# Preparing nine weight blocks in the last steps of five pairs of heads and in the last pair, and not every four steps of the last three

## The chip, the cores and the metric

One core of a Trainium2 chip runs the whole program. The metric is the device time of one execution in microseconds, as the median of several runs. The engines are TensorE (PE: matrix products and transposes; PEld is its weight load), VectorE (DVE), ScalarE (ACT), GpSimd (POOL), and SyncE (SP), which issues the DMAs of this kernel.

## The reference

Three layers, one after the other, in float32:

```python
# attention: q, k, v are (2, 8, 768, 64), centroids (8, 16, 64)
q_assign = argmax(q_n @ c_n.T); k_assign = argmax(k_n @ c_n.T)      # nearest of 16 centroids
scores = where(q_assign == k_assign, scale * q @ k.T, -1e9)
x = softmax(scores) @ v                                             # -> (1536, 512)
# first MoE layer: d_model 512, d_ff 2048
h = x @ w_in
P = a0 + a1*h + a2*h**2 + a3*h**3;  Q = 1 + |b0|*|h| + |b1|*h**2
y = (P / (Q + 1e-6)) @ w_out
# second MoE layer: d_ff 1536
g = y @ w_gate;  out = (silu(g) * (y @ w_val)) @ w_o2
```

## The kernel before, in words

The program is written as one order of instructions for each engine; nothing is reordered afterwards, and a tile that is taken again makes its first writer wait for the last reader of the tile before.

**Attention.** There are 2 x 4 pairs of heads, and 12 steps to a pair: two halves of the queries, three blocks of 128 queries in each half, two heads. Step n runs from 0 to 95 over all pairs, and s = n mod 12 is the step within its pair. A step has, on TensorE, four score products into a bank pair (`scores`, L344 and L346; there are two such tiles), two products of the weighted sum of an earlier half (`weighted`, L411) and six transposes of the probabilities of the step before the last (`transposes`, L400; three PSUM tiles); on VectorE the row maximum (`maximum`, L354); on ScalarE the exponential with its row sum (`exponentials`, L362), and the copies of the transposes to SBUF (L405), the second of which goes to VectorE in the steps `dve_evac = (2, 8, 10, 11)` (L403). At the start of a half come the reciprocals of the row sums (L369, L372), which go through DRAM and come back as a broadcast (`bring_back`, L388, at s = 4 and 10).

**Work for later, in `background(n, engine)`**, called at the end of each step for "dma", "pe", "dve", "pool" and "act" in this order. It puts into the steps of one pair what the next pair needs: on GpSimd, at s = 0 to 7, the split of its queries and keys in a high and a low part (`q_hi` L249, `q_scale` L254, `q_lo` L260, `k_hi` L264, `k_lo` L268, for two heads); on VectorE, at s = 0 to 6, the mask from the nearest centroids (`to_tokens` L284, `largest` L298, `reached` L303, `weigh` L309, `first_reached` L312, `one_hot` L315, `mask_values` L321, `to_rows` L329, which issues eight DMAs); on SP, at s = 10, two loads of v (L173) and the four query and key loads of the pair after the next (`load_qk`, L162). The last pair has none of this.

**Weight blocks.** The MoE needs 68 blocks of 128 x 512 weights that arrive as 64-bit floats. A block takes a load on SP (`block_start`, L65, 512 KB), a shift on ScalarE (`block_shift`, L70), a shift and a merge on VectorE (`block_bits_1` L79, `block_bits_2` L83), and a high and a low part on GpSimd (`block_hi` L89, `block_lo` L94). During attention the raw, shifted and merged tiles have one buffer each, so that the load of a block waits on SP's queue for the merge of the block before. Nine blocks are prepared during attention; the other 59 during the MoE, at a pace that is counted from nine.

**MoE.** Products of 128 x 512 (`product` L601, `project` L677) with the elementwise work between them. It begins with block 0 while the last half of attention is still being finished.

Of the kernel before, what the change touches and what calls it, by code (L numbers as in the profile page):

```python
# [20 lines left out]
def tile_kernel(ctx, tc, q_t, k_t, q_s, k_s, v_l, cent, w_in, w_out, a_co, b_co, w_gate, w_val, w_o2, out):  # L21
# [46 lines left out]
    def block_shift(t):  # L68
        t["u"] = pools["u"].tile([P, DM], F32, tag="u", name="u")
        nc.scalar.activation(out=t["u"], in_=t["high"], func=AF.Prelu, scale=2.0**-112, alpha=2.0**32)  # L70
# [5 lines left out]
    def block_bits_1(t):  # L76
        t["c"] = pools["c"].tile([P, DM], F32, tag="c", name="c")
        cb = t["c"].bitcast(U32)
        nc.vector.tensor_single_scalar(out=cb, in_=t["u"].bitcast(U32), scalar=3, op=ALU.logical_shift_left)  # L79

    def block_bits_2(t):
        cb = t["c"].bitcast(U32)
        nc.vector.scalar_tensor_tensor(  # L83
            out=cb, in0=t["low"].bitcast(U32), scalar=29, in1=cb, op0=ALU.logical_shift_right, op1=ALU.bitwise_or
        )

    def block_hi(t, w, on_pool=False):
        if on_pool:
            nc.gpsimd.tensor_scalar(out=w[:, 0, :], in0=t["c"], scalar1=1.0, scalar2=0.0, op0=ALU.mult, op1=ALU.add)  # L89
        else:  # L90
            nc.scalar.copy(out=w[:, 0, :], in_=t["c"])  # L91

    def block_lo(t, w):
        nc.gpsimd.tensor_tensor(out=w[:, 1, :], in0=t["c"], in1=r32(w[:, 0, :]), op=ALU.subtract)  # L94
# [10 lines left out]
    started = []  # L105
    ready = [0]

    def block_start():
        n = len(started)
        if n < len(loads):  # L110
            key, f, src = loads[n]
            started.append(block_load(src[f]))

    def block_slot(n):
        key, f, _ = loads[n]
        s = n % (WA + WX + WB)
        if WA <= s < WA + WX:
            wt_of[key, f] = x_in.tile([P, 2, DM], F32R, tag="x", name="w")
        else:
            wt_of[key, f] = (w_a if s < WA else w_pools["b"]).tile([P, 2, DM], F32R, tag="w", name="w")  # L120
        return wt_of[key, f]
# [36 lines left out]
    def load_qk(b, h):  # L158
        t = heads.setdefault((b, h), {})
        for key, src in (("xq", q_t), ("xk", k_t)):  # L160
            t[key] = x_tile(key)
            nc.sync.dma_start(out=t[key], in_=src[b, h])  # L162


    def load_pair(b, hp):
        for key, src in (("sq", q_s), ("sk", k_s)):
            live[key] = xs_p.tile([P, S], F32, tag=key, name=key)
            nc.sync.dma_start(out=live[key], in_=src[b, hp])

    def load_v(b, h):  # L170
        t = heads[b, h]
        t["v"] = v_p.tile([P, NB, D], F32, tag="v", name="v")
        nc.sync.dma_start(out=t["v"], in_=v_l[b, h])  # L173
# [34 lines left out]
    for g in range(4):  # L208
        r = slice(32 * g, 32 * g + 32)
# [36 lines left out]
    def q_hi(b, h):  # L246
        tiles_qk(b, h)
        t = heads[b, h]
        nc.gpsimd.tensor_scalar(out=t["q1"], in0=t["xq"], scalar1=scale, scalar2=0.0, op0=ALU.mult, op1=ALU.add)  # L249
        nc.sync.dma_start(out=r32(t["q2"])[0:D, :], in_=r32(t["q1"])[0:D, :])  # L250

    def q_scale(b, h):
        t = heads[b, h]
        nc.gpsimd.tensor_scalar(  # L254
            out=t["xq"][D:P, :], in0=t["xq"][D:P, :], scalar1=scale, scalar2=0.0, op0=ALU.mult, op1=ALU.add
        )

    def q_lo(b, h):
        t = heads[b, h]
        nc.gpsimd.tensor_tensor(out=t["q1"][D:P, :], in0=t["xq"][D:P, :], in1=r32(t["q1"][D:P, :]), op=ALU.subtract)  # L260

    def k_hi(b, h):
        t = heads[b, h]
        nc.gpsimd.tensor_scalar(out=t["k1"], in0=t["xk"], scalar1=1.0, scalar2=0.0, op0=ALU.mult, op1=ALU.add)  # L264

    def k_lo(b, h):
        t = heads[b, h]
        nc.gpsimd.tensor_tensor(out=t["k2"][0:D, :], in0=t["xk"][0:D, :], in1=r32(t["k1"][0:D, :]), op=ALU.subtract)  # L268


    def sims(b, hp):
        sim = live["sim"] = t_tile("sim").rearrange("p j c -> p (j c)")
        for m, key in enumerate(("sq", "sk")):
            x = live.pop(key)
            for half in range(2):
                g = 64 * m + 32 * half
                nc.tensor.matmul(
                    sim[g:g + 32, :], ct[:, hp, :, :], x[:, half * HALF:(half + 1) * HALF], start=True, stop=True,
                    tile_position=(0, g),
                )  # L280
# [45 lines left out]
    def to_rows(b, hp):  # L326
        del live["t1"], live["mx"]
        t3 = as_p.tile([P, HALF], F32, tag="t1", name="t3")
        nc.vector.transpose(out=t3, in_=live.pop("sm").rearrange("p j c -> p (j c)"))  # L329
        for e in range(2):  # L330
            for m, key in enumerate(("q2", "k2")):
                for half in range(2):
                    g = 64 * m + 32 * half + NC * e
                    nc.sync.dma_start(
                        out=r32(heads[b, 2 * hp + e][key])[D:KM, half * HALF:(half + 1) * HALF], in_=t3[g:g + NC, :]
                    )
# [144 lines left out]
        load_qk(pairs[1][0], 2 * pairs[1][1] + e)  # L481

    dve_evac = (2, 8, 10, 11)
    n_early, every = 9, 4
    early0 = 60
    XS, BB = 3, 4
    pv = []

    def background(n, engine):

        if n >= early0 - 3 and not started and engine == "dma":
            block_start()
        j, r = divmod(n - early0, every)
        if 0 <= j < n_early:
            if engine == "act" and r == 0:
                block_shift(started[j])
            elif engine == "dve" and r == 1:
                block_bits_1(started[j])
            elif engine == "dve" and r == 2:
                block_bits_2(started[j])  # L500
            elif engine == "dma" and r == 1 and j + 1 < n_early:
                block_start()
            elif engine == "pool" and r == every - 1:
                w = block_slot(j)
                block_hi(started[j], w, on_pool=True)
                block_lo(started[j], w)
                ready[0] += 1
        k, s = divmod(n, 2 * PER)
        if k + 1 < len(pairs):
            b, hp = pairs[k + 1]  # L510
            a, c = (b, 2 * hp), (b, 2 * hp + 1)
            d = s if k else s - 2
            if engine == "pool":
                for fn in {
                    0: [lambda: q_hi(*a), lambda: q_scale(*a)], 1: [lambda: q_lo(*a)], 2: [lambda: k_hi(*a)],
                    3: [lambda: k_lo(*a)], 4: [lambda: q_hi(*c), lambda: q_scale(*c)], 5: [lambda: q_lo(*c)],
                    6: [lambda: k_hi(*c)], 7: [lambda: k_lo(*c)],
                }.get(s, []):
                    fn()
            elif engine == "pe":  # L520
                if d == 0:
                    sims(b, hp)
            elif engine == "dve":
                steps = [[to_tokens], [largest], [reached], [weigh], [first_reached], [one_hot, mask_values]]
                for fn in steps[d] if 0 <= d < len(steps) else ():
                    fn()
                if d == len(steps):
                    to_rows(b, hp)
            elif engine == "dma" and s == XS and k + 2 < len(pairs):
                load_pair(*pairs[k + 2])  # L530
            elif engine == "dma" and s == 10:
                load_v(*a)
                load_v(*c)
                if k + 2 < len(pairs):
                    b, hp = pairs[k + 2]
                    load_qk(b, 2 * hp)
                    load_qk(b, 2 * hp + 1)
# [299 lines left out]
```

## Time and profile before

| | |
|---|---|
| three runs, median | 844.63 us (844.25 to 846.31) |
| the profiled execution | 844.0 us, span 842.2 us |
| TensorE busy | 807.8 us, 96% of the span |
| VectorE busy | 621.3 us, 74% |
| ScalarE busy | 450.1 us, 53% |
| GpSimd busy | 311.9 us, 37% |
| TensorE's granted clock, mean | 0.987 of full speed |

Busy shares are means over stages of different kind: attention ends some 260 us into the span. In the rows below a group of one instruction is a start time, a duration, engine, line, operation, what it writes and reads; in brackets stands the idle time of its engine before it and what ended it. The granted clock is a share of 2.4 GHz; the engine has two levels, 1.2 and 2.4 GHz, and a mean between them tells how long it was at either.

### The profile page before, as it was taken

How to read it: one execution, taken by the hardware profiler on the slowest of the kernel's cores; microseconds unless marked ns; L12 is line 12 of the kernel's file. 1: busy time of each engine (PE TensorE's matmuls, PEld its weight loads, DVE VectorE, ACT ScalarE, POOL GpSimd, SP SyncE). 2: the span in 40 equal slices, each digit the busy share in tenths (PEclk: the TensorE clock that was granted, in tenths of full speed). 3: DMA queues.
4: the chain of work that ended last, by engine and by line, in shares of the span. 5: the costliest groups of instructions: out<-in, count | busy, mean ns of one | idle time of the engine just before them, and what ended most of it. 6: DMA issues, size and time to landing. Idle time of an engine off the chain costs nothing.

```text
span 842.2 us, 11048 instructions
## 1 busy us (share of the span) xinstructions
PE 807.8 (96%) x3900; PEld 606.0 (72%) x3900; DVE 621.3 (74%) x929; ACT 450.1 (53%) x850; POOL 311.9 (37%) x274
## 2 busy tenths in 40 slices
PE   4999999999899999999999989999999999999998
PEld 3665566555466887777777767788888888888886
DVE  7776687677765999999999999985576555434435
ACT  5666776666486897667667666842432222211111
POOL 3566375465532333433333433321244323211112
PEclk8899999999899999999999999999999999999999
DMA  5255335435222211111111211122223121100004
GB/s 179 83 174 168 112 87 169 148 117 172 76 87 90 75 51 59 68 50 51 51 50 55 72 50 51 51 75 76 75 90 104 57 75 50 51 26 1 0 1 149
DMA packets 26550, 67.90 MB, mean 81 GB/s; under 512 B 4448, under 2 KB 9536, under 8 KB 26496
## 3 DMA queue, kind: packets, MB, share of 16 engines
q1 hardware_dynamic: 26496, 67.21, 24.4%
q8 instruction: 30, 0.49, 0.2%
q14 instruction: 24, 0.20, 0.1%
HBM read 59.48 MB, written 3.19 MB: 74 GB/s over the span
## 4 chain that ended last, share of the span: by engine, by line
PE 70%; DVE 22%; issue 3%; ACT 2%; POOL 1%; DMA 1%; SPq 0%; DVEq 0%; POOLq 0%; ACTq 0%
PE h_ps L601 29%; PE acc L677 17%; PE o_ps L411 8%; PE t_ps L400 8%; PE s_ps L344 4%; PE s_ps L346 3%; DVE g L634 3%; DVE part L695 3%; DVE td L640 3%; DVE td L637 2%; DVE tq L620 2%; DVE tp L623 2%; DVE c L79 1%; DVE c L83 1%; DVE st L354 1%
## 5 line engine op out<-in xcount | busy, mean ns | idle before, releaser
L601 PE MATMUL h_ps<-yhl,w 128*128 128x512 f32 x864 | 201.8, 389 | 0.0
L601 PEld LDWEIGHTS h_ps<-yhl,w 128*128 128x128 f32 x864 | 162.2, 188 | 33.7
L677 PE MATMUL acc<-g,w 128*128 128x512 f32 x576 | 144.9, 395 | 11.5 <-DVE part L695 6.8
L601 PE MATMUL h_ps<-xhl,w 128*128 128x512 f32 x576 | 138.8, 390 | 0.0
L677 PEld LDWEIGHTS acc<-g,w 128*128 128x128 f32 x576 | 106.2, 188 | 42.2 <-DVE part L695 10.8
L94 POOL TENSOR_TENSOR w<-c,w 128x512 fp32r<-128x512 f32 x68 | 92.9, 1368 | 108.5 <-ACT w L91 101.4
L601 PEld LDWEIGHTS h_ps<-xhl,w 128*128 128x128 f32 x576 | 107.9, 188 | 23.9 <-issue 1.2
L645 POOL TENSOR_TENSOR g<-td,tr 128x512 fp32r<-128x512 f32 x46 | 59.6, 1295 | 172.7 <-DVE td L640 151.8
L354 DVE TENSOR_REDUCE st<-s_ps 128x1 f32<-128x768 f32 x96 | 91.3, 952 | 32.1 <-PE s_ps L346 29.3
L405 ACT COPY pt<-t_ps 128x384 f32<-128x384 f32 x160 | 70.4, 482 | 68.7 <-PE t_ps L400 68.5
L695 DVE TENSOR_TENSOR part<-acc,part 128x512 f32<-128x512 f32 x74 | 48.6, 685 | 75.3 <-PE acc L677 75.2
L400 PEld LDWEIGHTS t_ps<-ident,p 128*128 128x128 f32 x576 | 63.5, 144 | 55.7 <-issue 42.1
L677 PE MATMUL acc<-w,g 128*128 128x512 f32 x432 | 103.3, 389 | 0.0
L362 ACT ACTIVATE p<-s_ps,st 128x768 f32<-128x768 f32 x96 | 87.5, 912 | 11.3 <-DVE st L354 8.1
L677 PEld LDWEIGHTS acc<-w,g 128*128 128x128 f32 x432 | 81.1, 188 | 16.8
L411 PE MATMUL o_ps<-pt,v 128*64 128x384 f32 x384 | 84.1, 519 | 3.6 <-DVE x L419 3.6
L400 PE MATMUL t_ps<-ident,p 128*128 128x128 f32 x576 | 86.0, 287 | 0.0
L692 ACT COPY ts<-acc 128x512 f32<-128x512 f32 x22 | 12.9, 588 | 111.4 <-PE acc L677 111.4
L693 POOL TENSOR_TENSOR part<-ts,part 128x512 f32<-128x512 f32 x22 | 30.3, 1394 | 111.9 <-ACT ts L692 111.8
L618 ACT ACTIVATE tq<-h_ps,babs 128x512 f32<-128x512 f32 x48 | 33.0, 688 | 68.9 <-PE h_ps L601 66.6
L344 PE MATMUL s_ps<-k,q 128*128 128x512 f32 x192 | 59.7, 393 | 2.8 <-ACT p L362 2.7
L83 DVE SCALAR_TENSOR_TENSOR c<-raw,c 128x512 uint32<-128x512 uint32 x68 | 57.2, 841 | 2.0
(101 smaller groups left out, 1049.4 us busy)
## 6 DMA issues: line engine op xcount, KB each, us to landing
raw<-w_in_dram SPq DMA_DIRECT2D x16, 512.0 KB, 3.6
raw<-w_out_dram SPq DMA_DIRECT2D x16, 512.0 KB, 3.3
raw<-w_gate_dram SPq DMA_DIRECT2D x12, 512.0 KB, 3.3
raw<-w_val_dram SPq DMA_DIRECT2D x12, 512.0 KB, 3.3
raw<-w_o_dram SPq DMA_DIRECT2D x12, 512.0 KB, 3.3
xq<-q_t_dram SPq DMA_DIRECT2D x14, 384.0 KB, 4.6
xk<-k_t_dram SPq DMA_DIRECT2D x14, 384.0 KB, 6.4
sq<-q_s_dram SPq DMA_DIRECT2D x8, 384.0 KB, 3.0
```

Source lines behind the costliest of these rows:

```text
L83: nc.vector.scalar_tensor_tensor(out=cb, in0=t["low"].bitcast(U32), scalar=29, in1=cb, op0=ALU.logical_shift_right, op1=ALU.bitwise_or)
L94: nc.gpsimd.tensor_tensor(out=w[:, 1, :], in0=t["c"], in1=r32(w[:, 0, :]), op=ALU.subtract)
L344: nc.tensor.matmul(s_ps[:, lo:hi], t["q1"][:, qs], t["k1"][:, lo:hi], start=True, stop=False)
L354: nc.vector.tensor_reduce(out=st[:, 0, k:k + 1], in_=live["s", b, hp, half, i, e], axis=AX.X, op=ALU.max, negate=True)
L362: nc.scalar.activation(out=p, in_=live.pop(("s", b, hp, half, i, e)), func=AF.Exp, bias=st[:, 0, k:k + 1], accum_out=st[:, 1, k:k + 1],)
L400: nc.tensor.transpose(t_ps[:, j, :], p[:, kb * P:(kb + 1) * P], ident)
L405: nc.scalar.copy(out=pt[:, ks, qc], in_=t_ps)
L411: nc.tensor.matmul(live["o", b, hp, half][e * D:(e + 1) * D, :], heads[b, 2 * hp + e]["v"][:, kb, :], live["pt", b, hp, half, e][:, kb, :] ...
L601: nc.tensor.matmul(h_ps, w[:, wi, cs], x[:, xi, cc, :], start=(n == 0), stop=(n == 3 * NCC - 1))
L645: spread.tensor_tensor(out=g[:, 1, :], in0=td, in1=tr, op=ALU.mult)
L677: nc.tensor.matmul(acc[c], lhs, rhs, start=(first and m == 0), stop=(last and m == 2))
L695: nc.vector.tensor_tensor(out=pt[:, c, :], in0=banks[c], in1=pt[:, c, :], op=ALU.add)
```

## The change

Before, the first load is issued at n = 57, and block j takes the four steps from n = 60 + 4j: shift, first bits, merge, GpSimd's two instructions, with the next load issued one step ahead of the merge. That puts three blocks into each of the last three pairs, at s = 0, 4 and 8. After it, a block has a start of its own, from a list, and takes three steps: shift at n0, first bits at n0 + 1, merge and GpSimd's two instructions at n0 + 2, and the next load is issued at n0 + 2 as well. Five blocks start at s = 8 of pairs 1 to 5 (n0 = 20, 32, 44, 56, 68), pair 6 has none, and four start at s = 0, 3, 6 and 9 of the last pair. The first load is issued at n = 17.

```diff
--- before.py
+++ after.py
@@ -481,26 +481,25 @@
         load_qk(pairs[1][0], 2 * pairs[1][1] + e)
 
     dve_evac = (2, 8, 10, 11)
-    n_early, every = 9, 4
-    early0 = 60
+
+    early = (20, 32, 44, 56, 68, 84, 87, 90, 93)
     XS, BB = 3, 4
     pv = []
 
     def background(n, engine):
 
-        if n >= early0 - 3 and not started and engine == "dma":
+        if n == early[0] - 3 and engine == "dma":
             block_start()
-        j, r = divmod(n - early0, every)
-        if 0 <= j < n_early:
-            if engine == "act" and r == 0:
+        for j, n0 in enumerate(early):
+            if engine == "act" and n == n0:
                 block_shift(started[j])
-            elif engine == "dve" and r == 1:
+            elif engine == "dve" and n == n0 + 1:
                 block_bits_1(started[j])
-            elif engine == "dve" and r == 2:
+            elif engine == "dve" and n == n0 + 2:
                 block_bits_2(started[j])
-            elif engine == "dma" and r == 1 and j + 1 < n_early:
+            elif engine == "dma" and n == n0 + 2 and j + 1 < len(early):
                 block_start()
-            elif engine == "pool" and r == every - 1:
+            elif engine == "pool" and n == n0 + 2:
                 w = block_slot(j)
                 block_hi(started[j], w, on_pool=True)
                 block_lo(started[j], w)
```

## Rows read from the trace of the kernel before

**Rows 1.** Windows: stretch, its length, busy time (instructions) of PE, PEld, DVE, ACT, POOL; PE clock, DMA, GB/s.
```profile
43.69:72.68 28.99, 28.99 (x180) 17.34 (x182) 21.37 (x31) 19.84 (x47) 16.37 (x16) 1.00 0.49 154
159.28:193.38 34.10, 31.07 (x180) 18.42 (x182) 26.44 (x37) 21.63 (x50) 21.73 (x22) 0.95 0.39 130
182.41:186.42 4.01, 4.01 (x16) 2.55 (x18) 1.36 (x2) 2.58 (x7) 3.46 (x4) 0.57 0.40 124
193.38:230.15 36.77, 32.00 (x180) 18.60 (x182) 27.41 (x37) 21.51 (x50) 22.25 (x23) 0.91 0.40 123
230.15:260.38 30.23, 30.23 (x187) 18.19 (x188) 18.98 (x32) 22.76 (x54) 9.23 (x13) 1.00 0.24 81
260.38:842.20 581.82, 566.62 (x2475) 458.98 (x2472) 431.82 (x640) 277.81 (x459) 173.29 (x133) 1.00 0.18 60
```

**Rows 2.** Timeline, DVE: starts of row maxima, steps 5, 6, 8, 11 of pair 5 and so on.
```profile
173.40 0.94 DVE L354 TENSOR_REDUCE st<-s_ps 128x1 f32<-128x768 f32 x1
...
178.75 0.94 DVE L354 TENSOR_REDUCE st<-s_ps 128x1 f32<-128x768 f32 x1
...
186.46 0.96 DVE L354 TENSOR_REDUCE st<-s_ps 128x1 f32<-128x768 f32 x1 [0.72 <-PE s_ps L346]
...
193.38 0.96 DVE L354 TENSOR_REDUCE st<-s_ps 128x1 f32<-128x768 f32 x1
...
251.14 0.96 DVE L354 TENSOR_REDUCE st<-s_ps 128x1 f32<-128x768 f32 x1
...
253.44 0.96 DVE L354 TENSOR_REDUCE st<-s_ps 128x1 f32<-128x768 f32 x1 [0.89 <-PE s_ps L346]
```

**Rows 3.** Timeline of the long step of pair 5.
```profile
175.63 1.88 POOL L260 TENSOR_TENSOR q<-xq,q 64x768 fp32r<-64x768 f32 x1
...
175.75 2.17 DVE L315 TENSOR_TENSOR sm<-wt,mx 128x384 f32<-128x384 f32 x1
...
179.78 0.90 ACT L362 ACTIVATE p<-s_ps,st 128x768 f32<-128x768 f32 x1 [2.35 <-DVE st L369]
```

**Rows 4.** Timeline: a block's instructions in steps 8 to 10 of pairs 5 and 7.
```profile
187.34 0.42 DVE L79 TENSOR_SCALAR c<-u 128x512 uint32<-128x512 uint32 x1
...
190.84 0.68 DVE L83 SCALAR_TENSOR_TENSOR c<-raw,c 128x512 uint32<-128x512 uint32 x1
...
251.37 0.67 ACT L70 ACTIVATE u<-raw 128x512 f32<-128x512 f32 x1
```

**Rows 5.** Timeline: SP's queue into pair 6; GpSimd's start in pairs 1 and 6.
```profile
49.36 0.83 POOL L249 TENSOR_SCALAR q<-xq 128x768 fp32r<-128x768 f32 x1 [15.29 <-PE s_ps L346]
...
51.45 1.96 DVE L303 TENSOR_TENSOR sm<-t,mx 128x384 f32<-128x384 f32 x1
...
191.58 0.35 SPq L65 DMA_DIRECT2D raw<-w_out_dram  x1
...
192.03 1.12 SPq L388 DMA_DIRECT2D rb<-rd  x2
...
194.30 0.42 SPq L162 DMA_DIRECT2D xq<-q_t_dram  x1
...
199.79 0.83 POOL L249 TENSOR_SCALAR q<-xq 128x768 fp32r<-128x768 f32 x1 [6.20 <-DMA xq<-q_t_dram]
```

**Rows 6.** Timeline of steps 2 to 5 of the last pair, and landing of block loads.
```profile
236.96 0.68 DVE L83 SCALAR_TENSOR_TENSOR c<-raw,c 128x512 uint32<-128x512 uint32 x1
...
237.67 0.34 SPq L65 DMA_DIRECT2D raw<-w_out_dram  x1
...
240.00 0.21 ACT L362 ACTIVATION_READ_ACCUMULATOR p<-s_ps,st 128x1 f32 x1
...
240.77 0.86 ACT L405 COPY pt<-t_ps 128x384 f32<-128x384 f32 x2 [0.56 <-PE t_ps L400]
...
243.12 0.60 PE L344 MATMUL s_ps<-k,q 128*128 128x512 f32 x2
...
DMA to landing us min/median/max: 3.2/3.3/5.1
```

## The prediction

> **What bounds the kernel now.** I read the page's table of slices first (TensorE is busy nearly throughout, so a gain has to come from places where it idles or runs slowly), then the starts of the row maxima, which mark one attention step each, and cut the span by them. [rows 1] is that cut, one pair of heads (12 steps) to a line. The pair from 43.69 takes 28.99 us, and the three after it 28.86, 28.89 and 28.85; TensorE is busy in all of it, at full clock. These four pairs prepare no weight block. The next two prepare three each and take 34.10 and 36.77 us, with TensorE idle for 3.0 and 4.8 us and a mean granted clock of 0.95 and 0.91. The last pair, with three blocks too and no query/key preparation, is again full: 30.23 us up to the first product of the MoE. From there to the end TensorE is busy in 566.6 of 581.8 us, so that whatever attention gives up is expected at the end of the kernel in full: the first products follow the last transposes on TensorE without a gap, and the loads that they need are counted by blocks (nine, before and after) and not by time.
>
> So the two pairs hold 34.10 - 28.87 = 5.23 and 36.77 - 28.87 = 7.90 us, together **13.13 us**, over the mean of the four free pairs. The trace shows where it goes (steps are counted from 0 within a pair). In pair 5 step 5 takes 5.35 us [rows 2] where a step takes 2.31: VectorE does block work, then its one-hot compare stands for 2.17 us beside GpSimd's subtraction for the next query (175.63 to 177.51), and the step's maximum comes only at 178.75, so that ScalarE waits 2.35 us for its exponential and TensorE runs dry [rows 3]. From 182.41 to 186.42, most of step 8, the mean granted clock is 0.57 [rows 1], near the lower of TensorE's two levels (1.2 of 2.4 GHz): that step pays again for a stall that is over. The third block of that pair lies in steps 8 to 11, where the mask work and the query/key work are done: from the maximum at 186.46 to that at 193.38, three steps, are 6.92 us [rows 2], which is 3 x 2.31. In them the shift left 0.42 and the merge 0.68 us on VectorE [rows 4]. This block costs nothing, and it is the very place to which five blocks go.
>
> **What the change removes.** All of the six blocks of pairs 5 and 6 but one, which stays in steps 8 to 11 of pair 5. Both pairs should come back to 28.87: -13.13 us. Nothing else is removed: the number of blocks, the instructions of each and the size of its load stay.
>
> **What it adds to pairs 1 to 5: a block in steps 8 to 10.** ScalarE's shift (0.67 us) falls behind an exponential, where ScalarE waits for transposes anyway: in the last pair it ran at 251.37, and the step around it, 251.14 to 253.44, was 2.30 us [rows 2, 4]. VectorE has in such a step the maximum (0.96) and at most one copy; that 0.42 or 0.68 more fit beside them is what the 6.92 us for three steps show. GpSimd's two instructions are issued one step earlier in the order, but wait for the merge as before, with nothing behind them until the next pair. Cost: 0. If that cover were gone, a block would cost the 0.67 + 0.42 + 0.68 of its own, which is 1.8 us; the row of three steps at 6.92 speaks for 0.
>
> **What moves with it: the load of the next block on SP's queue.** It goes out at step 10 and waits there for that step's merge, since there is one raw buffer. Behind it in the queue stand the v loads and the four query/key loads of the pair after next. The old order shows the price: in pair 5 the block load (191.58) came after the merge (190.84), then the broadcast of the reciprocals (1.12 us), and the query load left at 194.30, so that GpSimd's first instruction of pair 6 started at 199.79, 6.41 us into the pair [rows 5]. In the new order the broadcast is ahead of the wait, so the query load leaves some 1.1 us sooner: about 5.3 us into the pair (an estimate from these rows), now in each of pairs 2 to 6. Pair 1 has that lateness already: GpSimd started at 49.36, 5.67 us in, its late subtraction held VectorE's comparison for 1.96 us [rows 5], and the pair still took 28.99 us, 0.14 over the shortest. VectorE had the slack to catch up as no block was in its way, and so it will be in pairs 2 to 6 until step 8. Between nothing (a gain is excluded, TensorE being full) and the 7.90 us of pair 6, where late queries and blocks met, I take 0.1 for each of five: **+0.5 us**, by the row that is nearest in lateness.
>
> The Trainium skill speaks against the change at this point ("SBUF — State Buffer", section "SBUF: two separate sides"): VectorE with two SBUF inputs and GpSimd reading SBUF exclude each other for a whole instruction. By that rule the trace agrees, with 1.96 us for the comparison; what the lock would make of the time if it were not recovered is the second rival.
>
> **What it adds to the last pair: one block more, every three steps.** The merge of a block is now one step before the shift of the next, where two lay between, and the load sits in that gap. In the old trace a merge at step 2 ran at 236.96, its load was issued at 237.67 and the median landing is 3.3 us later, at 240.97 [rows 4, 6]. ScalarE would want it for the shift once the exponential of step 3 has read out, 240.00 + 0.21 = 240.21: a wait of 0.76, and then 0.67 for the shift, ending 241.64. The two copies due at 240.77 (0.86 us) end at 242.50 and not 241.63, the next exponential (0.90) at 243.4, and the score product that needs its bank is due at 243.12 [rows 3, 6]: 0.3 us late. The block after it has its merge in a step without a copy on VectorE, a little sooner, and does not wait; the last one waits as much, but no score products follow. I take **+0.4 us**. Bounds: nothing, or every load at the longest landing, 5.1 us [rows 6]: 1.8 us more of waiting, so some 2.1 us late for the first, and as much or less for the other two, 4 to 5 us with the lower clock that a dry TensorE brings.
>
> **The end of attention.** The last block's merge is one step later, in front of the last reciprocal; 0.68 us of VectorE at most, where VectorE waits for TensorE. I take **+0.1**, bounds 0 and 0.7.
>
> **Sum.** -13.13 + 0.5 + 0.4 + 0.1 = -12.1 us. The profiled execution took 844.0 us (span 842.2), so 831.9 for it; the median of the three runs lies 0.6 above, so **832.5 us**, 1.4% less. Differences within 0.3% (2.5 us) I call no change.
>
> **The rivals.** (1) *The loads of the last pair come too late.* Three waits of ScalarE take the place of the stalls removed. For it: one raw buffer, and a step between merge and shift. Against: the median landing leaves only 0.76 us. With the longest landings, 832.5 + 4.5 = 837. (2) *The lock in each pair.* GpSimd's late subtraction holds VectorE in pairs 2 to 6 and nothing is recovered: at most the whole 1.96 us each, 9.8 in all, and 844.6 - 13.1 + 9.8 + 0.5 = 841.8. Against: pair 1, which had that and kept its 28.99. (3) *A block costs the same wherever it is.* Six blocks cost 13.13, 2.19 each; five in pairs 1 to 5 cost 10.9, and the time is 844.6 - 13.1 + 10.9 + 0.5 = 842.9, no change. Against: the 6.92 us of three steps with a block. (4) *Slower: SP's queue holds the query loads in five pairs.* If late queries alone, and not the blocks, made pair 6 what it was, each of pairs 2 to 6 loses 7.90: 844.6 - 13.1 + 39.5 + 0.5 = 871.5. It decides from 13.13 / 5 = 2.6 us a pair on. For it: pair 6 is the one with 6.41 us of lateness, and it lost more than pair 5. Against: pair 1 at 5.67 lost 0.14.
>
> **How the numbers follow.** Forecast 0.77, rivals (1) 0.09, (2) 0.05, (3) 0.04, (4) 0.05. Faster are the forecast, (1) and (2): 0.91; same is (3), 0.04; slower is (4), 0.05. The range runs from 830.5 (none of the added terms, 844.25 - 13.13 = 831.1, and 0.6 for the spread of the runs) to 838, which takes in rival (1) and a late-query loss of up to 1.2 us a pair; 0.86 lies in it.
>
> **What would show it.** In the new profile: pairs 5 and 6 at 28.8 to 29.1 us and clock 1.00 (right), pairs 1 to 5 with steps 9 to 11 at 6.9 us; GpSimd's first instruction some 5 us into pairs 2 to 6, with a comparison of about 2 us and no longer pair; in the last pair ScalarE waiting for the raw tile at the second and fourth of its blocks, under 1 us each; TensorE never at the lower level between 45 and 260 us. Wrong would be: a pair from 2 to 6 over 30 us (rival 2 or 4), or a last pair over 33 us (rival 1), or attention ending 12 us sooner with the end of the kernel not following.

## The result and the profile after

The changed kernel takes **833.5 us** (median of 4 runs, 832.29 to 837.14) against 844.44 for the kernel before in the same series (4 runs, 842.42 to 846.31): ratio 0.9878, 95% interval 0.9839 to 0.9917, some 1.2% less. The prediction was 832.5. The time is close, but it comes about differently than the prediction had it: the removal was worth 0.2 us more than said, one of the added terms was nothing, and another was seven to eleven times what was said.

The profiled execution of the changed kernel is the longest of its four, 837.14 us with a span of 835.4, so a second profiled one (e1 below, 835.99, span 834.2) stands beside it. Windows of the changed kernel, with the columns of [rows 1]: pairs 1, 5, 6, the last pair up to the first product of the MoE, step 8 of that pair, and all that follows:

```profile
42.46:71.32 28.86, 28.86 (x180) 17.32 (x182) 21.86 (x33) 20.40 (x48) 18.07 (x18) 1.00 0.51 162
157.90:186.75 28.85, 28.85 (x180) 17.31 (x182) 22.20 (x32) 20.39 (x48) 18.25 (x19) 1.00 0.48 150
186.75:215.62 28.87, 28.87 (x180) 17.33 (x182) 21.00 (x31) 19.75 (x47) 16.45 (x17) 1.00 0.41 129
215.62:250.14 34.52, 32.24 (x187) 19.14 (x188) 20.13 (x34) 23.19 (x55) 10.75 (x14) 0.95 0.18 58
236.71:240.34 3.63, 3.49 (x16) 2.36 (x18) 2.10 (x5) 2.21 (x6) 1.55 (x3) 0.68 0.00 1
250.14:835.40 585.26, 568.15 (x2475) 459.92 (x2472) 431.90 (x639) 277.66 (x459) 173.59 (x134) 0.99 0.17 59
```

What to see: pairs 5 and 6, which were 34.10 and 36.77 us [rows 1], are as long as every other pair, with TensorE busy in all of each and at full clock. Pair 1 now has a block, and VectorE, ScalarE and GpSimd are each busier than in [rows 1]; its length is not. The six pairs together went from 186.46 to 173.16 us: **-13.30**, against the one profiled execution of the kernel before. The stall has moved to the last pair, 30.23 before and 34.52 now (32.95 in e1): **+4.3 and +2.7**. TensorE idles in it for 34.52 - 32.24 = 2.28 us in either execution; here a step at a mean granted clock of 0.68 comes on top.

The other differences of the two profiled executions are 0.06 us at the start, -1.29 in pair 0, whose code is unchanged and which took 26.64 in e1 (26.44 before), and +3.44 after attention, where a stretch of 9.4 us at the hand-over between two layers ran at 0.82 of the clock. That stretch is no more than half of it: TensorE was busy 1.5 us longer in that part and idle 1.9 us longer, and what made it idle was not followed. e1 has 583.50 for that part and e2, e3 and e4 have 581.7 to 581.8, as before [rows 1], with the same MoE code. So the sum for this execution is 0.06 - 1.29 - 13.30 + 4.29 + 3.44 = -6.8, its span being 835.4 after 842.2. Without the difference after attention, as in most of the profiled executions, what is left is -13.3 + 2.7 to 4.3: -10.6 to -9.0 us. The medians differ by 10.9, and by 9.8 in the series of e1 (842.76 and 832.93).

The timeline of a block in the last three steps of pair 5 (the first row maximum of these steps, ScalarE's shift, and the first maximum of pair 6: time, duration, engine, line):

```profile
179.84 0.96 DVE L354 TENSOR_REDUCE st<-s_ps 128x1 f32<-128x768 f32 x1
...
180.06 0.67 ACT L70 ACTIVATE u<-raw 128x512 f32<-128x512 f32 x1
...
186.75 0.96 DVE L354 TENSOR_REDUCE st<-s_ps 128x1 f32<-128x768 f32 x1
```

Three steps with a block take 6.91 us, as in [rows 2] (6.92). The row at 186.46 there begins step 9, not step 8, and the shift of that block (185.80) ran just ahead of it, in the slow step 8; here the shift lies within the three steps. The timeline of SP's queue ahead of pair 3, and of the late start of GpSimd in pair 2, which begins at 71.32:

```profile
76.59 0.83 POOL L249 TENSOR_SCALAR q<-xq 128x768 fp32r<-128x768 f32 x1 [5.07 <-DMA xq<-q_t_dram]
...
79.08 1.59 DVE L303 TENSOR_TENSOR sm<-t,mx 128x384 f32<-128x384 f32 x1
...
97.64 0.68 DVE L83 SCALAR_TENSOR_TENSOR c<-raw,c 128x512 uint32<-128x512 uint32 x1
...
98.38 0.35 SPq L65 DMA_DIRECT2D raw<-w_in_dram  x1
...
99.72 0.42 SPq L162 DMA_DIRECT2D xq<-q_t_dram  x1
```

The queue is as predicted: the block's load leaves after the merge, and the query load of the pair after next 1.3 us behind it. GpSimd starts 5.27 us into pair 2 and 4.58, 5.22, 5.51 and 4.53 into pairs 3 to 6 ([rows 5]: 6.41 into pair 6 before). No pair is longer for it. VectorE's comparison takes 1.59 us beside GpSimd's late work, and 0.55 in the pairs in which it meets none; the rule that the prediction took from the Trainium skill ("SBUF — State Buffer", section "SBUF: two separate sides") agrees with that row, and costs nothing here, as VectorE makes it good before its block comes at step 8.

The last pair (timeline; steps of 2.30, 2.42, 2.83, 1.94, 2.90, 2.25, 2.30, 4.15, 3.63, 2.87 and 2.41 us). In brackets: the wait, and what ended it:

```profile
223.28 0.33 SPq L65 DMA_DIRECT2D raw<-w_in_dram  x1
...
226.91 0.67 ACT L70 ACTIVATE u<-raw 128x512 f32<-128x512 f32 x1 [1.08 <-DMA raw<-w_in_dram]
...
229.63 0.33 SPq L65 DMA_DIRECT2D raw<-w_out_dram  x1
...
235.14 0.66 ACT L70 ACTIVATE u<-raw 128x512 f32<-128x512 f32 x1 [1.85 <-DMA raw<-w_out_dram]
...
235.90 0.43 DVE L79 TENSOR_SCALAR c<-u 128x512 uint32<-128x512 uint32 x1 [2.38 <-ACT u L70]
...
236.24 0.55 DVE L419 TENSOR_TENSOR x<-o_ps,rb 128x384 f32<-128x384 f32 x1
...
236.85 0.94 PE L411 MATMUL o_ps<-pt,v 128*64 128x384 f32 x4 [1.91 <-DVE x L419]
...
240.24 0.34 SPq L65 DMA_DIRECT2D raw<-w_in_dram  x1
...
244.21 0.67 ACT L70 ACTIVATE u<-raw 128x512 f32<-128x512 f32 x1 [0.28 <-DMA raw<-w_in_dram]
```

Read it from the bottom of the stall upwards. TensorE's weighted products (L411) wait 1.91 us for the normalisation of the half before (L419, VectorE), which frees their bank. VectorE had nothing long to do there: its next instruction in order was the block's first bits (L79), which waited 2.38 us for ScalarE's shift, and the normalisation was queued behind it. The shift in turn waited 1.85 us for its load, issued 5.5 us sooner. The chain is load, shift, first bits, normalisation, products.

### The profile page after: what moved, and what is told of

Same layout as the page of the kernel before. It is cut to its first block, busy times and chain, and to the rows that moved or that the text cites. A ratio compares the mean times of both kernels' runs of the same rounds, so it can differ in the third digit from the quotient of the medians.

```text
span 835.4 us, 11054 instructions
## 1 busy us (share of the span) xinstructions
PE 804.5 (96%) x3900; PEld 604.6 (72%) x3900; DVE 614.6 (74%) x929; ACT 449.8 (54%) x850; POOL 311.7 (37%) x274
## 4 chain that ended last, share of the span: by engine, by line
PE 70%; DVE 22%; issue 3%; ACT 2%; DMA 1%; POOL 0%; DVEq 0%; POOLq 0%; ACTq 0%
PE h_ps L600 28%; PE acc L676 16%; PE o_ps L411 9%; PE t_ps L400 8%; PE s_ps L344 4%; PE s_ps L346 4%; DVE g L633 3%; DVE part L694 3%; DVE td L639 3%; DVE td L636 3%; DVE tq L619 2%; DVE tp L622 2%; DVE c L79 1%; DVE tp L623 1%; PE sim L277 1%
## 5 line engine op out<-in xcount | busy, mean ns | idle before, releaser
L411 PE MATMUL o_ps<-pt,v 128*64 128x384 f32 x384 | 82.9, 514 | 2.0 <-DVE x L419 1.9
L692 POOL TENSOR_TENSOR part<-ts,part 128x512 f32<-128x512 f32 x22 | 30.2, 1393 | 111.9 <-ACT ts L691 111.9
L661 ACT ACTIVATE sg<-h_ps 128x512 f32<-128x512 f32 x36 | 21.6, 601 | 67.6 <-PE h_ps L600 67.6
```

Source lines behind the costliest of these rows:

```text
L411: nc.tensor.matmul(live["o", b, hp, half][e * D:(e + 1) * D, :], heads[b, 2 * hp + e]["v"][:, kb, :], live["pt", b, hp, half, e][:, kb, :] ...
```

## The experiments

**The theory:** the lost 2.7 to 4.3 us of the last pair are late loads: one raw buffer and one step between a merge and the next shift, and what they stop is VectorE's queue. **Rivals:** an accident of that one execution; the fourth block as such; the narrow spacing of the instructions even with loads in time. A second question is whether the place of the block in a pair (steps 8 to 11) is what brought the 13.3 us, or only that there is one block in a pair.

**e1. The changed kernel once more**, unaltered, timed six times.

> The changed kernel once more, unaltered, for a second profile and a steadier time. Theory (the shifts of the last pair wait for loads that are issued one step before they are needed): the last pair is again 3 to 5 us longer than the 30.2 us it took before the change, with ScalarE waiting for the raw tile in front of the second, third and fourth shift. Rival (one long landing of 5.5 us by chance): the last pair is within 1 us of 30.2. Pairs 1 to 6 at 28.85 to 28.9 us under both. Time about 833 us; the handover between the two MoE layers may or may not show the lower clock.

832.93 us (831.52 to 835.99, 6 runs), ratio to before 0.9879 (0.9855 to 0.9903). Windows of its last pair and of the rest, then the timeline of the last three shifts and of the products that wait:

```profile
217.75:250.70 32.95, 30.67 (x187) 18.29 (x188) 20.16 (x34) 23.11 (x55) 10.78 (x14) 1.00 0.19 61
250.70:834.20 583.50, 568.16 (x2475) 460.07 (x2472) 431.69 (x639) 277.88 (x459) 173.39 (x134) 1.00 0.18 59
```

```profile
229.08 0.67 ACT L70 ACTIVATE u<-raw 128x512 f32<-128x512 f32 x1 [1.12 <-DMA raw<-w_in_dram]
...
237.27 0.66 ACT L70 ACTIVATE u<-raw 128x512 f32<-128x512 f32 x1 [1.79 <-DMA raw<-w_out_dram]
...
238.98 0.93 PE L411 MATMUL o_ps<-pt,v 128*64 128x384 f32 x4 [1.85 <-DVE x L419]
...
245.63 0.69 ACT L70 ACTIVATE u<-raw 128x512 f32<-128x512 f32 x1 [1.14 <-DMA raw<-w_in_dram]
```

The same waits at the same places: an accident is out, though 32.95 is just under the 3 to 5 us over 30.2 that the theory had. The third load again takes longest, 5.5 us from issue to shift against 3.7 for the two beside it. The stall is the same 2.28 us; the lower clock is absent, and 34.52 - 32.95 = 1.6 us is what it added in the first execution.

The DMA view around that third load shows what was late about it (what was moved in each of 40 equal slices of the window, then one of the queues: packets, MB, share of the 16 engines). First 229 to 236 us of the first execution, then 231.5 to 238.5 us of e1:

```profile
GB/s 0 0 0 0 0 0 0 0 0 234 94 234 374 351 398 328 468 281 117 23 0 0 23 0 23 0 23 23 23 23 23 23 0 0 0 0 0 0 0 0
q8 instruction: 1, 0.02, 0.8%
```

```profile
GB/s 0 0 0 0 0 0 0 211 304 47 117 304 304 492 351 374 258 141 0 23 0 0 23 0 23 23 23 23 47 0 0 0 0 0 0 0 0 0 0 0
q8 instruction: 1, 0.02, 1.0%
```

Most of the 512 KB has moved 2.8 us after the issue; the last sixteenth follows in pieces of 4 KB (23 GB/s for one slice) over some 2 us more. In both executions one packet of 16 KB on the queue that the profile calls "instruction" lies within the load, and it does in e4, whose third load has such a tail, a shorter one. Two loads that were viewed alone and without such a packet (the one issued at 246.01 in the last pair before, and e3's at 232.96) have no tail; in e2 the packet comes behind the data and there is none either. So the largest wait is a load that is issued late and, at the same place each time, held up on its way; that the packet holds it is read from these views and was not tested by an edit. At the median landing of 3.3 us [rows 6] it would have landed at 232.9, ahead of ScalarE, which was ready at 235.14 - 1.85 = 233.29. Of e1's 2.7 us some 2.0 lie in steps 7 to 9, behind this load (9.02 us, in e3 below 7.03), and 0.6 in step 4, behind the second (2.94, in e3 2.31).

**e2. The merge one step sooner in the last pair**, so that the load has two steps again. Timed five times.

```diff
             elif engine == "dve" and n == n0 + 1:
                 block_bits_1(started[j])
+                if n0 >= 84:
+                    block_bits_2(started[j])
-            elif engine == "dve" and n == n0 + 2:
+            elif engine == "dve" and n == n0 + 2 and n0 < 84:
                 block_bits_2(started[j])
-            elif engine == "dma" and n == n0 + 2 and j + 1 < len(early):
+            elif engine == "dma" and n == n0 + (1 if n0 >= 84 else 2) and j + 1 < len(early):
```

> As the changed kernel, but in the last pair the merge follows the first bits in the same step (n0 + 1), and the next load is issued there: two steps and not one between a load and the shift that needs it, with four blocks as before. Theory (late loads): the waits for the raw tile shrink to under 0.5 us, the last pair comes back to 30.2 to 31 us and the time falls by 3 to 4 us, to about 829.5. Rival (the fourth block's own work on ScalarE and VectorE): the last pair stays at 34 to 35 us, and the time at 833.

831.48 us (831.1 to 833.07, 5 runs), ratio 0.9862 (0.9837 to 0.9887). Windows as for e1, then VectorE's timeline in step 1:

```profile
215.77:247.50 31.73, 30.42 (x187) 18.27 (x188) 20.04 (x34) 23.43 (x55) 10.88 (x14) 1.00 0.19 63
247.50:829.30 581.80, 566.64 (x2475) 458.83 (x2472) 431.71 (x639) 278.07 (x459) 173.41 (x133) 1.00 0.18 60
```

```profile
219.40 0.43 DVE L79 TENSOR_SCALAR c<-u 128x512 uint32<-128x512 uint32 x1 [0.36 <-ACT u L70]
...
219.86 0.69 DVE L83 SCALAR_TENSOR_TENSOR c<-raw,c 128x512 uint32<-128x512 uint32 x1
...
220.47 0.55 DVE L419 TENSOR_TENSOR x<-o_ps,rb 128x384 f32<-128x384 f32 x1
```

No shift waits for its load any more, and the last pair loses 1.2 us against e1, but it is 31.73 and not 30.3. The rest is of the edit's own making, and of the same kind: first bits and merge now stand together ahead of the normalisation, in steps 1 and 7 (2.86 and 2.93 us, where others take 2.3).

**e3. Three blocks, four steps apart, in the last pair; the sixth block in steps 8 to 10 of pair 6.** Timed four times.

```diff
-    early = (20, 32, 44, 56, 68, 84, 87, 90, 93)
+    early = (20, 32, 44, 56, 68, 80, 84, 88, 92)
```

> Three blocks in the last pair, four steps apart, and the ninth in steps 8 to 10 of pair 6: starts 20, 32, 44, 56, 68, 80, 84, 88, 92. The wait of a load for the merge is still one step later in the order than before the change. Theory (late loads): a load has two steps before its shift, the last pair comes back to 30.2 to 30.8 us, pair 6 stays at 28.9, and the time is about 829 us, the same as with the merge a step sooner. Rival (the fourth block): the same 829 us, since that block has left the last pair; the next run tells the two apart.

**830.85 us** (830.67 to 832.05, 4 runs), ratio 0.9852 (0.9827 to 0.9876): the lowest median of the versions timed several times, though 2.1 us under e1 is within the 0.3% that the prediction calls no change. Windows of pair 6, the last pair and the rest:

```profile
188.23:217.09 28.86, 28.86 (x180) 17.32 (x182) 20.99 (x33) 20.32 (x48) 18.28 (x19) 1.00 0.38 121
217.09:247.34 30.25, 30.25 (x188) 18.20 (x188) 18.98 (x32) 22.79 (x54) 9.24 (x13) 1.00 0.22 73
247.34:829.10 581.76, 566.40 (x2475) 458.89 (x2472) 431.68 (x639) 278.08 (x459) 173.25 (x133) 1.00 0.18 60
```

The sixth pair takes a block for nothing as well, and the last pair is full again, at 30.25 us ([rows 1]: 30.23).

**e4. Three blocks, but three steps apart.** One run.

```diff
-    early = (20, 32, 44, 56, 68, 84, 87, 90, 93)
+    early = (20, 32, 44, 56, 68, 80, 84, 87, 90)
```

> Three blocks in the last pair again, but three steps apart: starts 20, 32, 44, 56, 68, 80, 84, 87, 90. Theory (late loads): the second and third shift wait for their loads as in the changed kernel, and the last pair is 33 to 34.5 us. Rival (the fourth block): with three blocks the last pair is at 30.2 to 30.8 us, as when they are four steps apart.

832.46 us. Window of the last pair, then the two shifts that wait:

```profile
216.71:248.69 31.98, 30.64 (x187) 18.29 (x188) 19.17 (x32) 22.65 (x54) 9.31 (x13) 1.00 0.21 69
```

```profile
228.23 0.68 ACT L70 ACTIVATE u<-raw 128x512 f32<-128x512 f32 x1 [1.44 <-DMA raw<-w_out_dram]
...
235.25 0.66 ACT L70 ACTIVATE u<-raw 128x512 f32<-128x512 f32 x1 [0.62 <-DMA raw<-w_in_dram]
```

As many blocks as e3 and the last pair 1.73 us longer, less than the 33 to 34.5 us expected: it is the distance, not the number.

**e5. The changed kernel without the last three loads.** Blocks 7 to 9 take the raw values of block 6, which lie there already; all their arithmetic runs. What it computes from those weights is not the reference's. One run.

```diff
-            started.append(block_load(src[f]))
+            if n in (6, 7, 8):
+                started.append(dict(low=started[5]["low"], high=started[5]["high"]))
+            else:
+                started.append(block_load(src[f]))
```

> As the changed kernel with four blocks three steps apart in the last pair, but the loads of the last three of them are left out: their shift and merge read the raw tile of the block before them, so that no shift waits for a transfer (those three weights are wrong, all instructions stay). Theory (late loads): the last pair, which took 34.5 and 33.0 us, comes to 30.2 to 30.8 us. Rival (the fourth block's own work on ScalarE and VectorE): it stays over 31.5 us.

832.09 us. Window of the last pair:

```profile
217.54:247.98 30.44, 30.36 (x187) 18.25 (x188) 20.17 (x34) 23.29 (x55) 10.78 (x14) 1.00 0.04 14
```

Four blocks three steps apart, with nothing to wait for, take 30.44 us. So the fourth block and the narrow spacing cost 0.2 us over three blocks, and the late loads 32.95 - 30.44 = 2.5 us in e1 and 34.52 - 30.44 = 4.1 in the first execution, its lower clock included.

**e6 and e7. One block in each of pairs 1 to 5, but in steps 4 to 6, or 0 to 2** (the rest as e3). One run each.

```diff
-    early = (20, 32, 44, 56, 68, 84, 87, 90, 93)
+    early = (16, 28, 40, 52, 64, 80, 84, 88, 92)   # e6
+    early = (12, 24, 36, 48, 60, 80, 84, 88, 92)   # e7
```

> Five blocks in steps 4 to 6 and not 8 to 10 of pairs 1 to 5, else as with three blocks four apart in the last pair: starts 16, 28, 40, 52, 64, 80, 84, 88, 92. Theory (what cost 13.1 us before was the place: block work of VectorE meeting the mask work and GpSimd's query work): pairs 1 to 5 rise from 28.86 to 30 to 33 us each, 6 to 20 us in all, with a long step 5 or 6. Rival (a block costs nothing anywhere as long as there is one to a pair; three to a pair was too many): all pairs stay at 28.9 us.

> The same five blocks in steps 0 to 2 of pairs 1 to 5: starts 12, 24, 36, 48, 60, 80, 84, 88, 92. Theory (the place): pairs 1 to 5 at 29 to 31 us, dearest where the merge in step 2 stands in front of a comparison that GpSimd's subtraction holds up. Rival (the number to a pair): 28.9 us each.

837.73 and 833.34 us. Windows of pair 5 of e6, and of pair 4 of e7:

```profile
162.49:192.75 30.26, 29.26 (x180) 17.41 (x182) 21.60 (x33) 20.42 (x48) 18.10 (x18) 1.00 0.49 152
```

```profile
130.50:160.46 29.96, 28.93 (x180) 17.32 (x182) 22.23 (x32) 20.34 (x48) 18.37 (x18) 1.00 0.44 140
```

Pairs 1 to 5 take 30.13, 29.58, 29.97, 29.97 and 30.26 us in e6 (+1.12 each over 28.86) and 29.95, 28.99, 29.08, 29.96 and 29.81 in e7 (+0.70). The same block is free in steps 8 to 10. The place matters, but five blocks at 1.12 make 5.6 us, just under the 6 to 20 expected and less than half of what the six in pairs 5 and 6 cost before. Nor is all of the 1.12 surely the block's: e6's pair 6 has no block before step 8 and took 29.51 us. GpSimd started 2.19 us into it, and VectorE's one-hot compare stood beside GpSimd's subtraction:

```profile
205.96 1.82 POOL L260 TENSOR_TENSOR q<-xq,q 64x768 fp32r<-64x768 f32 x1
206.23 1.96 DVE L315 TENSOR_TENSOR sm<-wt,mx 128x384 f32<-128x384 f32 x1
```

**e8. Query, key and v loads issued one step later** (starts as e3), to see what a late query costs by itself. One run.

```diff
-            elif engine == "dma" and s == 10:
+            elif engine == "dma" and s == 11:
```

> Blocks as with three in the last pair four apart (8 to 10 of pairs 1 to 6), but the v, query and key loads of each pair are issued one step later, at step 11: GpSimd then starts some 7.5 us into pairs 2 to 7 and not 5. Theory (late queries alone cost nothing while VectorE has no block in steps 0 to 7): pairs 2 to 6 at 28.9 to 29.2 us. Rival (SP's queue and the late queries made pair 6 of the kernel before as long as it was, 36.77 us): pairs 2 to 6 at 30 us or more each.

830.4 us. The start of pair 2, and GpSimd's first instruction in it:

```profile
72.02 0.96 DVE L354 TENSOR_REDUCE st<-s_ps 128x1 f32<-128x768 f32 x1
...
77.17 0.83 POOL L249 TENSOR_SCALAR q<-xq 128x768 fp32r<-128x768 f32 x1 [4.93 <-DMA xq<-q_t_dram]
```

GpSimd starts 5.15 us into the pair, no later than in the changed kernel: nothing else of SP's stands between the two places in the program, so that SP's order of instructions is that of e3. The loads did not move, and the run is in effect a second execution of e3 (last pair 30.24 us). The other runs answer its question in part, as GpSimd's start varies from pair to pair: with a block in steps 8 to 10 only, e1's pair 4 (6.08 us in) took 28.86 us and e3's pair 5 (6.32) 28.89; the longest such pair with a start past 4.4 us was e3's pair 1 (5.90), at 29.23.

**e9 and e10. Two blocks in pair 5 (steps 0 and 4), and three (0, 4 and 8).** Fewer in the pairs ahead of it, the last four as e3. **e11: two blocks in pair 6**, behind one in steps 8 to 10 of pair 5. One run each.

```diff
-    early = (20, 32, 44, 56, 68, 84, 87, 90, 93)
+    early = (20, 32, 44, 60, 64, 80, 84, 88, 92)   # e9
+    early = (20, 32, 60, 64, 68, 80, 84, 88, 92)   # e10
+    early = (20, 32, 44, 68, 72, 76, 84, 88, 92)   # e11
```

> Two blocks in pair 5, at its steps 0 and 4, none in pair 4 and none in steps 8 to 11 of pair 5; else as with three in the last pair four apart: starts 20, 32, 44, 60, 64, 80, 84, 88, 92. One block to a pair cost 0.70 us at step 0 and 1.12 us at step 4 on average. If these add, pair 5 takes 28.86 + 1.8 = 30.7 us. Theory (two together hold up one step after the other until TensorE runs dry and drops to the lower clock): 32 to 34 us, with a step 5 over 5 us and a slow step 7 or 8.

> Pair 5 alone as it was before the change, with blocks at steps 0, 4 and 8: starts 20, 32, 60, 64, 68, 80, 84, 88, 92. Theory (the third block is free): the pair is within 0.5 us of that with two blocks, and at 32 to 34.5 us if two compound. Rival (three are what is too many): 1 us or more over the pair with two.

> Blocks at steps 0 and 4 of pair 6, with a block in steps 8 to 10 of pair 5 ahead of it, so that the query loads of pair 6 wait for a merge as they did before the change: starts 20, 32, 44, 68, 72, 76, 84, 88, 92. If late queries add to the two blocks, pair 6 is 1 us or more over the pair with two blocks of the run with starts 60 and 64 (before the change pair 6 took 2.67 us more than pair 5). If they do not, both take the same within 0.5 us.

834.4, 833.33 and 837.49 us. Windows: pair 5 of e9 and its step 8; pair 5 of e10; pair 6 of e11:

```profile
158.51:191.57 33.06, 30.77 (x180) 18.27 (x182) 24.47 (x35) 21.08 (x49) 20.70 (x20) 0.95 0.52 168
180.50:184.65 4.15, 4.02 (x16) 2.49 (x18) 1.50 (x3) 2.21 (x6) 3.98 (x5) 0.59 0.40 134
```

```profile
158.47:189.65 31.18, 29.21 (x180) 17.36 (x182) 25.16 (x36) 21.64 (x50) 22.62 (x22) 1.00 0.49 156
```

```profile
187.57:222.34 34.77, 31.28 (x180) 18.40 (x182) 26.26 (x35) 20.99 (x49) 20.83 (x21) 0.95 0.42 137
```

e10 against e9: the third block, in steps 8 to 10, adds nothing; the pair with three is the shorter one, which neither expectation had, mainly because it kept the full clock. Two blocks cost 31.18 - 28.86 = 2.3 us (singly 0.70 + 1.12 = 1.8). e9 has the same long steps 5 and 6 (4.60 and 3.00 us, in e10 4.61 and 3.00) and then a step 8 of 4.15 us at clock 0.59, where e10's takes 2.62 at 1.00: 1.5 of the 33.06 - 31.18 = 1.9 us more. In e11 GpSimd starts 5.99 us into the pair, as the block load ahead holds the queries back, and 3.96 us into e9's; two blocks there cost 34.77 - 28.86 = 5.9 us, 1.7 more than in e9 at the same mean clock. VectorE's two comparisons (L303, L315) took 2.19 and 2.17 us in e11, and 1.10 and 1.17 in e9. That lateness as such costs this is not shown: these are single runs of two different pairs, and GpSimd's start alone does not order the pairs. With a block in steps 0 to 2 (e7), a start at 1.76 us gave 29.96, at 3.26 28.99 and at 6.30 29.95; e6's pair 6 lost 0.65 with an early start. So late queries alone cost 0 to 0.4 us; what they add beside two blocks stays open, with 1.7 us as the one measurement.

## Why the prediction was right, and where it was not

**The removal, -13.13: measured -13.30**, in both executions of the changed kernel. That the steps 8 to 10 hold a block at no cost was the step that carried it, and e6, e7 and e10 show that it is the place: the pairs with the same block lose 1.12 us with it in steps 4 to 6, 0.70 in steps 0 to 2. A small slip: 28.87 is the mean of three of the four free pairs; of all four it is 28.90, and the sum 13.07. What the prediction took as one sum splits by e9 to e11 into three parts: the two blocks in steps 0 to 6 (2.3 us in a pair), the lower clock after the stall (1.5 in e9), and what e11 has on top (1.7, its cause open). Pair 6 of the kernel before lost 7.90 us; 2.0 us of its 36.77 over e11's 34.77 were not separated. The pair 5 of before (34.10) has blocks in the same steps as e10's (31.18); 1.6 of the difference are step 8 (4.19 and 2.62 us), the rest was not separated. As the lower clock came in e9 and not in e10, what there was to remove may differ from one execution of the kernel before to the next; one was profiled.

**Late queries, +0.5: measured 0.** Lateness of 4.5 to 5.5 us in pairs 2 to 6 (4.4 to 6.1 in e1) was forecast well (about 5.3), and VectorE recovered it entirely. Rivals 2 (the lock) and 4 (SP's queue) fall with that; rival 3 (a block costs the same anywhere) by the pairs of 28.86 us with a block in them.

**The last pair, +0.4: measured +4.3 and +2.7.** This is the term that failed; the mechanism was named, as rival (1), and its size was bounded at 4 to 5 us, but the value taken was near the wrong end. The first wait was about as worked out (1.08 and 1.12 us for 0.76). Two steps of the working were wrong. "The block after it ... does not wait": it waited 1.85 and 1.79 us, since its load took 5.5 us from issue to shift, where the working had the median landing of 3.3; at the median there would have been no wait, as forecast, and the tail of the load (e1) is what was missed. And the price of a wait was followed only along ScalarE, to the copies and the next score product. VectorE's first bits also wait for the shift, and the normalisation, which TensorE needs, is queued behind them; that is where the 1.91 us came from. The prediction's own test, a last pair over 33 us for rival 1, is met by the first execution and just missed by e1.

**The end of attention, +0.1** lies within the window of the last pair; e5 bounds it, together with the fourth block, at 0.2.

**The sum.** With the measured terms it is 844.0 - 13.3 + 2.7 = 833.4 for the profiled execution of before, or 834.0 beside the median, against the 832.5 that stands on record and 833.5 and 832.93 measured. That the forecast is so near is in part luck: its last pair was 2.2 us or more too low (+0.5 for it and the end of attention, +2.7 and +4.3 measured), and the queries and the removal gave 0.7 us of it back (+0.5 that did not come, and 0.2 more removed). "TensorE never at the lower level between 45 and 260 us" was wrong for one execution of two. That the end of the kernel follows the end of attention was right: e3, without the wait in the last pair, has that pair at 30.25 and the rest at 581.76 us.

## What to carry to other kernels

Before a background task is moved, look for the steps of the period in which the engines it uses have no other work: here one block was free in a third of the pair, and pairs with it at the two other places tried were 0.7 to 1.1 us longer. When a wait is added, follow each engine that waits for it, not only the first: the costly instruction was one queued behind a cheap one that waited for the late one. And with a single buffer, the distance between the last reader and the next use must hold the longest landing of the trace, not the median; four steps did (e3), three did not (e4).

## What the runs showed of the hardware

The same stall does not always bring the lower clock. In the last pair of the changed kernel TensorE idled 2.28 us in each of two executions; one had a step at a mean of 0.68 behind it, the other stayed at 1.00, 1.6 us apart. e9 and e10 have the same two long steps and 2.29 and 1.97 us of idle time, near but not equal; the clock fell to 0.59 in the one and stayed at 1.00 in the other. The part after attention took 581.7 to 581.8 (e2 to e4), 583.5 (e1) and 585.3 us (the first execution) with one and the same code, the last with a stretch of 9.4 us at 0.82, e1 with one of 10 us at 0.84.

The third load of the last pair took 5.5 us from issue to shift in both executions of the changed kernel, at a DMA share of 0.18 and 0.19 over the pair, where its neighbours of the same size took 3.6 to 4.0. Its last sixteenth came some 2 us behind the rest, with one 16 KB packet of the "instruction" queue within it (the views under e1). No run moved that packet.
